# K and V loads of an attention decode kernel, each made as two DMAs of 64 partitions

## The chip, the cores and the metric

The kernel runs on one core of one Trainium2 chip. The metric is the time of one execution on the device in microseconds (us); of several runs the median is given. A profiled execution has a time of its own, and its span (from the first to the last instruction) is a little shorter than that time.

The core has five engines that run side by side and wait for one another by semaphores: TensorE (PE, its weight loads PEld), VectorE (DVE), ScalarE (ACT), GpSimd (POOL) and SyncE (SP). In this kernel SyncE does nothing but wait and issue transfers. The transfers are done by 16 DMA engines, which move data from the main memory (HBM) to the on-chip memory (SBUF). SBUF has 128 partitions.

## The reference

The inputs are one token for each of 8 sequences (x, 640 wide), a cache of 4096 keys and values for each of 32 heads (128 wide), and weights. What is computed, in short:

```python
xn = layernorm(x)
q  = (xn @ wq) as 32 heads of 128
scores = einsum("bhqd,bhkd->bhqk", q, k_cache) * 128 ** -0.5
o  = einsum("bhqk,bhkd->bhqd", softmax(scores), v_cache) @ wo
y  = layernorm(xn)
h  = gelu(y @ w1 + b1)
out = x + o + (h @ w2 + b2)
```

All tensors are bfloat16. The two caches are 8 x 32 x 4096 x 128 values each, 268 MB a cache; everything else is small beside them.

## The kernel before, in words

The work is cut into 32 tiles. A tile is one sequence with 8 of the 32 heads; `i` counts the tiles. For a tile, the keys of 8 heads are laid on the 128 partitions: 16 partitions for a head, and on each partition 256 keys of 128 values, 65,536 bytes that lie in one piece in HBM. `cache_src` makes this view of the cache. So the K load of a tile is one DMA of 128 rows of 64 KB (8.39 MB), and its V load is another.

SBUF holds three such tiles, the three slots of `S_sb`: K loads go to slots `KA` and `KB` in turn, V loads always to `VS`. Each slot has one load semaphore, `ld_s[s]`. A DMA adds 16 to its semaphore when all of it has landed; the helper `_Dma.sig` counts these 16 and returns the ticket (semaphore and value) for which a reader waits.

What is done with a tile:

- K: for 176 of the 256 keys of a partition, VectorE multiplies the keys by the query in place, folds them once and sums them, in three chunks (`dve_chunk`). For the other 80 keys TensorE transposes them, ScalarE copies the result out of PSUM, and TensorE multiplies it by the query (`pe_T`, `act_T`, `pe_QK`); VectorE picks out the right head (`dve_sel`). TensorE does not wait for the load itself: GpSimd waits (`k_ready`) and writes a small flag, `kr_sb`, whose ticket TensorE waits for.
- Then VectorE takes the maximum of each head (`dve_max`), and ScalarE makes the 8 exponentials (`act_exp`).
- V: TensorE multiplies the 256 slices of V by the probabilities (`pe_PV`), one tile behind.

SyncE issues the loads in the order of the positions in `at`: K of the next tile at `o - 51`, V of this tile at `o + 50` (lines 871 and 872), so K and V in turn. Ahead of a load, SyncE waits until its slot is free. In `load_k` (line 368) that is, from tile 6 on, the end of the exponentials of tile i - 2. In `load_v` (line 383) it is the end of the PV matmuls of tile i - 1. All loads from SyncE go through one queue. The V load of the last tile but one (i = 30) is made in two pieces along the keys, cut at 192 of 256 (`V_CUT`); the second piece has a semaphore of its own, `ld_vl`, for which `pe_PV` waits ahead of slice 192.

The program first records the calls of every engine in a list and then emits them, VectorE, ScalarE and TensorE as loops, in which the values they wait for grow by a constant step from turn to turn. Line 111 emits every instruction, which is why the profile gives that line for all of them.

Ahead of the first tile come the load of wq (into slot `VS`), two layer norms and the query. Behind the last K tiles, the weights of the MLP and wo are loaded into the K slots, and the products with them are added up in one PSUM bank.

Of the kernel before, what the change touches and what calls it, by code (L numbers as in the profile page):

```python
# [14 lines left out]
P = 128  # L15
# [177 lines left out]
def bass_parallel_sum__gqa_block_cached__mixer_channel_mlp__decode_kernel(  # L193
# [19 lines left out]
    NKEY = SK * HS // P  # L213
# [21 lines left out]
    KA, KB, VS = 0, 1, 2  # L235
# [2 lines left out]
    NL = 3  # L238
    WN_CUT = (0, 5 * CT, 7 * CT, 7 * CT + CT // 2, HS * CT)
    V_CUT = (0, 192, 256)  # L240

    def jp_of(i):
        return 80
# [6 lines left out]
    def kslot(i):  # L250
        return KA if i % 2 == 0 else KB
# [8 lines left out]
    with ExitStack() as es:  # L260
# [5 lines left out]
        tile = [S_sb[:, s, :].rearrange("p (j d) -> p j d", d=DH) for s in range(3)]  # L266
# [6 lines left out]
        def scratch(n, rows=P, slot=KB):  # L273
# [73 lines left out]
        pe, dve, act, sp, pool = (_Eng(sem(f"{n}_s")) for n in ("pe", "dve", "act", "sp", "pool"))  # L347
        pe2, act2, fin, fin2 = (_Eng(sem(n)) for n in ("pe2_s", "act2_s", "fin_s", "fin2_s"))
        ld_s = [_Dma(sem(f"ld_s{s}")) for s in range(3)]
        ld_x, ld_b1, ld_b2, ld_wq, ld_w1, ld_w2a, ld_w2b, st_a, st_o = (  # L350
            _Dma(sem(n)) for n in ("ld_x", "ld_b1", "ld_b2", "ld_wq", "ld_w1", "ld_w2a", "ld_w2b", "st_a", "st_o"))
        ld_vl = [_Dma(sem(f"ld_vl{q}")) for q in range(1, len(V_CUT) - 1)]
        ld_wl = [_Dma(sem(f"ld_wl{q}")) for q in range(2)]
        ld_wn = [_Dma(sem(f"ld_wn{q}")) for q in range(len(WN_CUT) - 1)]
        tk = {}
# [8 lines left out]
        def cache_src(cache, i):  # L364
            hq, b = divmod(i, B)
            return cache[b, hq * HS:(hq + 1) * HS].rearrange("h (p j) d -> (h p) j d", j=NKEY)

        def load_k(i):
            s = kslot(i)
            if i >= KLATE:  # L370
                sp.wait(tk[("exp", i - 2)])
            elif i >= 2:
                sp.wait(tk[("kt", i - 2)], tk[("km", i - 2)])
            elif s == KB:
                sp.wait(tk["qT"])
            tk[("k", i)] = ld_s[s].sig(sp.dma_start(tile[s], cache_src(A_k_cache, i)))

        def load_mlp():
            sp.wait(tk[("kt", NQ - 2)], tk[("km", NQ - 2)])
# [3 lines left out]
        def load_v(i):  # L383
            sp.wait(tk["qmm"] if i == 0 else tk[("pv", i - 1)])
            if i != NQ - 2:
                tk[("v", i)] = [ld_s[VS].sig(sp.dma_start(tile[VS], cache_src(A_v_cache, i)))]
                return
            tk[("v", i)] = []
            for d, lo, hi in zip([ld_s[VS]] + ld_vl, V_CUT[:-1], V_CUT[1:]):
                if lo:  # L390
                    d.n += 1
                tk[("v", i)].append(
                    d.sig(sp.dma_start(tile[VS][:, lo:hi, :], cache_src(A_v_cache, i)[:, lo:hi, :])))

# [324 lines left out]
        def pe_PV(i):  # L719
            PVB.use(pe)  # L720
            pe.wait(tk[("exp", i)])
            for j in range(NKEY):
                if j == 0:
                    pe.wait(tk[("v", i)][0])
                elif j in V_CUT:
                    pe.wait_ge(ld_vl[V_CUT.index(j) - 1].sem, 1)
                last = pe.matmul(PV_ps[:, 0:HS], tile[VS][:, j, :], P_sb[:, :, j],
# [114 lines left out]
        at(NQ * Q - 55, load_mlp)  # L842
        at(NQ * Q - 54.9, load_w2b)
        at(-870, load_k, 0)
        at(NQ * Q - 60.1, zero_w2b)
        at(-800, consts_pool)
# [20 lines left out]
        for i in range(NQ):  # L867
            o = i * Q
            last = i == NQ - 1
            if i:  # L870
                at(o - 51, load_k, i)
            at(o + 50, load_v, i)
            at(o - 52, qrep, i)
            at(o - 2, k_ready, i)
            at(o - 11, pe_qbc, i)
            at(o - 10.5, act_qbc, i)
            nt = jp_of(i) // TPB
            w = 42.0 / nt
            for t in range(nt):
                at(o + w * t, pe_T, i, t)  # L880
                at(o + w * (t + 0.4), act_T, i, t)
                at(o + w * (t + 1.5), pe_QK, i, t)
            at(o + 2, dve_chunk, i, 0)
            at(o + 26, dve_chunk, i, 1)
            at(o + 52, dve_sel, i, 0)
            at(o + 55, dve_sel, i, 1)
            at(o + 58, dve_chunk, i, 2)
            at(o + 84, dve_max, i)
            at(o + 90 if i else o + Q + 45, act_exp, i)
            at(o + Q + 48, pe_RS, i)  # L890
            at(o + Q + 57, dve_rinv, i)
            at(o + Q + 50, pe_PV, i)
            if not last:
                at(o + Q + 71, act_O, i)
            at(o + Q + 75, o_norm, i)
# [81 lines left out]
```

## Time and profile before

| what | value |
|---|---|
| time, median of 3 runs | 1281.42 us (1281.33 to 1281.44) |
| time of the profiled execution | 1281.24 us |
| its span | 1279.9 us |
| SyncE's waits ahead of V loads, for the PV matmuls | 785.6 us in 31 waits |
| SyncE's waits ahead of K loads, for the exponentials | 310.3 us in 26 waits |
| GpSimd's flag, waiting for K loads | 295.2 us in 31 waits |
| PV matmuls, waiting for V loads | 138.3 us in 30 waits |
| VectorE, waiting for K loads | 126.9 us in 28 waits |
| K load, from issue to landing | 26.1 to 39.1 us, median 38.8 |
| V load, from issue to landing | 24.7 to 52.6 us, median 31.6 |

How to read it: in the profile's names, `S_sb<-in_A_k_cache_dram` is a K load into one of the slots, `S_sb<-in_A_v_cache_dram` a V load, and `SPq` is SyncE's sequencer as it issues. The DMA row has one digit for each fortieth of the span, in tenths of busy time. "q1" is the DMA queue that SyncE fills, and its share is the time of its packets as a share of 16 DMA engines' span; a packet's time holds the time in which it is under way. A wait is put down to what ended last.

### The profile page before, as it was taken

What the parts mean: (1) busy time and instruction counts of PE and PEld (TensorE: products, weight loads), DVE (VectorE), ACT (ScalarE), POOL (GpSimd) and SP (SyncE); (2) the same over time, 40 slices, a digit from 0 to 9 for tenths busy, and PEclk for the clock granted to TensorE, in tenths of its full rate; (3) what the DMA queues carried; (4) which work ended last, traced back from release to release, by engine and by line L of the source; (5) the groups of instructions that cost most, each with busy time, mean ns of one, the idle gap of its engine ahead of it and who ended that gap; (6) DMA issues with size and microseconds to landing.
All of it is one profiled execution on the core that took longest, in us unless ns stands there. A gap on an engine that the chain in (4) does not pass through costs nothing.

```text
span 1279.9 us, 34138 instructions
## 1 busy us (share of the span) xinstructions
PE 672.1 (53%) x13794; PEld 570.6 (45%) x13794; DVE 1103.0 (86%) x684; ACT 476.5 (37%) x906; POOL 109.6 (9%) x121
## 2 busy tenths in 40 slices
PE   2536555446645446545456554456454466464476
PEld 0435444435535345444345444345343355353465
DVE  2899998889888889888899888898888898888894
ACT  0524444233444233443234443234443334442331
POOL 0020010000000000000000000000000000000050
PEclk8656655565565556555555555555565556655665
DMA  9999999999999999999999999999999999999998
GB/s 424 425 431 429 434 434 428 440 434 430 432 438 428 438 432 432 434 432 434 430 440 430 432 434 438 428 432 436 430 438 432 432 432 440 426 434 436 426 444 365
DMA packets 10784, 551.97 MB, mean 431 GB/s; under 512 B 1242, under 2 KB 1523, under 8 KB 1812
## 3 DMA queue, kind: packets, MB, share of 16 engines
q1 hardware_dynamic: 10736, 551.79, 99.7%
q8 instruction: 8, 0.13, 0.0%
q14 instruction: 4, 0.03, 0.0%
q10 hardware_dynamic: 36, 0.02, 0.0%
HBM read 551.80 MB, written 0.01 MB: 431 GB/s over the span
## 4 chain that ended last, share of the span: by engine, by line
DMA 46%; DVE 37%; issue 12%; ACT 4%; PE 1%; DVEq 0%; SPq 0%
DMA S_sb<-in_A_k_cache_dram 42%; DVE S_sb L111 26%; DVE Sd_sb L111 8%; ACT P_sb L111 4%; DMA S_sb<-in_B_w_dram 2%; DMA S_sb<-in_A_wo_dram 2%; DVE S_ps L111 1%; PE TR_ps L111 1%; DVE mx_sb L111 1%; DVE mxT_sb L111 0%; DVE mbT_sb L111 0%; DVEq L109 0%; DVE mq_sb L111 0%; DVE NB_sb L111 0%; DVE ri_sb L111 0%
## 5 line engine op out<-in xcount | busy, mean ns | idle before, releaser
L111 PE MATMUL TR_ps<-ident_bf,S_sb 128*128 128x128 bf16 (+1 forms) x2578 | 341.8, 279 | 354.1 <-POOL kr_sb L111 331.4
L111 DVE TENSOR_TENSOR S_sb<-S_sb,qbc_sb 128x7552 bf16<-128x7552 bf16 (+1 forms) x96 | 388.8, 4050 | 127.2 <-DMA S_sb<-in_A_k_cache_dram 126.9
L111 PEld LDWEIGHTS TR_ps<-ident_bf,S_sb 128*128 (+2 forms) x2578 | 245.1, 103 | 412.4 <-issue 339.6
L111 DVE TENSOR_REDUCE Sd_sb<-S_sb 128x59 f32<-128x3776 bf16 (+1 forms) x96 | 390.2, 4065 | 6.0
L111 ACT ACTIVATE KT_sb<-TR_ps 128x1024 bf16<-128x1024 bf16 x320 | 326.6, 1023 | 120.5 <-PE TR_ps L111 109.4
L111 PE MATMUL PV_ps<-P_sb,S_sb 128*128 128x8 bf16 x8192 | 224.0, 175 | 141.3 <-DMA S_sb<-in_A_v_cache_dram 138.3
L111 PEld LDWEIGHTS PV_ps<-P_sb,S_sb 128*128 128x128 bf16 x8192 | 221.4, 103 | 144.1 <-DMA S_sb<-in_A_v_cache_dram 141.0
L111 DVE TENSOR_TENSOR S_sb<-S_sb 128x3776 bf16<-128x3776 bf16 (+1 forms) x96 | 206.5, 2151 | 3.3
L111 ACT ACTIVATE P_sb<-Sd_sb,NB_sb 128x256 bf16<-128x256 f32 x256 | 126.3, 494 | 210.1 <-DVE NB_sb L111 210.1
L111 PE MATMUL S_ps<-qrep_sb,KT_sb 128*128 128x8 bf16 x2560 | 121.9, 177 | 50.3 <-ACT KT_sb L111 47.0
L111 ACT ACTIVATE oU_sb<-PV_ps 128x8 f32<-128x8 f32 x31 | 5.5, 177 | 377.5 <-PE PV_ps L111 377.5
L111 PEld LDWEIGHTS S_ps<-qrep_sb,KT_sb 128*128 128x128 bf16 x2560 | 91.8, 103 | 82.2 <-ACT KT_sb L111 40.0
L111 POOL TENSOR_TENSOR oT_sb<-oU_sb,ri_sb 128x8 bf16<-128x8 f32 x31 | 71.5, 2306 | 371.4 <-DVE S_sb L111 315.3
L111 POOL COPY qrep_sb<-qT_sb 128x128 bf16<-128x128 bf16 x32 | 18.5, 578 | 470.0 <-PE S_ps L111 453.3
L111 ACT ACTIVATION_READ_ACCUMULATOR P_sb<-Sd_sb,NB_sb 128x1 f32 x256 | 47.7, 186 | 0.0
L111 DVE TENSOR_TENSOR S_ps<-S_ps,mask_sb 128x320 f32<-128x320 f32 (+1 forms) x65 | 31.6, 486 | 2.7 <-PE S_ps L111 2.7
L111 DVE TENSOR_REDUCE Sd_sb<-S_ps 128x40 f32<-128x320 f32 x64 | 31.5, 492 | 2.2
L111 ACT ACTIVATE qbc_sb<-QB_ps 128x128 bf16<-128x128 f32 x32 | 8.9, 277 | 58.2 <-PE QB_ps L111 58.2
L111 PE MATMUL QB_ps<-ident_bf,qrep_sb 128*128 128x128 bf16 x32 | 9.1, 283 | 40.2 <-DVE S_sb L111 21.9
L111 POOL MEMSET kr_sb<- 128x1 f32 x32 | 3.1, 98 | 295.2 <-DMA S_sb<-in_A_k_cache_dram 295.2
L111 PEld LDWEIGHTS QB_ps<-ident_bf,qrep_sb 128*128 128x128 bf16 x32 | 3.3, 103 | 43.1 <-ACT oU_sb L111 29.1
L111 PE MATMUL CH_ps<-rs_sb,ones_f 128*128 128x8 f32 x64 | 16.2, 326 | 6.1 <-ACT P_sb L111 6.1
(70 smaller groups left out, 150.1 us busy)
## 6 DMA issues: line engine op xcount, KB each, us to landing
S_sb<-in_A_v_cache_dram SPq DMA_DIRECT2D x1, 6144.0 KB, 26.8
S_sb<-in_A_wq_dram SPq DMA_DIRECT2D x1, 5120.0 KB, 15.2
S_sb<-in_A_wo_dram SPq DMA_DIRECT2D x1, 2560.0 KB, 18.4
S_sb<-in_B_w_dram SPq DMA_DIRECT2D x1, 2160.0 KB, 30.3
S_sb<-in_B_w_dram SPq DMA_DIRECT2D x1, 2080.0 KB, 34.8
S_sb<-in_A_v_cache_dram SPq DMA_DIRECT2D x1, 2048.0 KB, 31.3
S_sb<-in_A_wo_dram SPq DMA_DIRECT2D x1, 1280.0 KB, 21.1
S_sb<-in_A_wo_dram SPq DMA_DIRECT2D x1, 800.0 KB, 22.6
```

The costliest lines, as they stand in the source:

```text
L111: inst = getattr(e, name)(*a, **k)
```

## The change

Each K load and each V load becomes two DMAs, the first for partitions 0 to 63 (the first four heads of the tile), the second for partitions 64 to 127 (the other four). Both add 16 to the slot's semaphore, and `load_rows` returns the ticket of the second, so readers wait for both. The two are issued one after the other by SyncE, with no wait between them. Of the V load of tile 30, the first piece (keys 0 to 191 of a partition) is made as two DMAs too; the second piece stays one DMA of 128 partitions. Nothing else is changed.

```diff
+    PH = P // 2
...
+        def load_rows(s, cache, i, lo, hi):
+            for r in range(0, P, PH):
+                t = ld_s[s].sig(sp.dma_start(
+                    tile[s][r:r + PH, lo:hi, :], cache_src(cache, i)[r:r + PH, lo:hi, :]))
+            return t
+
         def load_k(i):
             s = kslot(i)
...
-            tk[("k", i)] = ld_s[s].sig(sp.dma_start(tile[s], cache_src(A_k_cache, i)))
+            tk[("k", i)] = load_rows(s, A_k_cache, i, 0, NKEY)
...
         def load_v(i):
             sp.wait(tk["qmm"] if i == 0 else tk[("pv", i - 1)])
             if i != NQ - 2:
-                tk[("v", i)] = [ld_s[VS].sig(sp.dma_start(tile[VS], cache_src(A_v_cache, i)))]
+                tk[("v", i)] = [load_rows(VS, A_v_cache, i, 0, NKEY)]
                 return
-            tk[("v", i)] = []
-            for d, lo, hi in zip([ld_s[VS]] + ld_vl, V_CUT[:-1], V_CUT[1:]):
-                if lo:
-                    d.n += 1
+            tk[("v", i)] = [load_rows(VS, A_v_cache, i, 0, V_CUT[1])]
+            for d, lo, hi in zip(ld_vl, V_CUT[1:-1], V_CUT[2:]):
+                d.n += 1
                 tk[("v", i)].append(
                     d.sig(sp.dma_start(tile[VS][:, lo:hi, :], cache_src(A_v_cache, i)[:, lo:hi, :])))
```

## The prediction

> **What bounds the kernel now.** I read first the head of the page and its DMA rows, to see whether any compute engine or the transfers fill the span.
>
> ```profile
> span 1279.9 us, 34138 instructions
> PE 672.1 (53%) x13794; PEld 570.6 (45%) x13794; DVE 1103.0 (86%) x684; ACT 476.5 (37%) x906; POOL 109.6 (9%) x121
> ...
> DMA  9999999999999999999999999999999999999998
> ...
> DMA packets 10784, 551.97 MB, mean 431 GB/s; under 512 B 1242, under 2 KB 1523, under 8 KB 1812
> ...
> q1 hardware_dynamic: 10736, 551.79, 99.7%
> ```
>
> No slice of the DMA row falls below 8 tenths, and the one queue that SyncE fills (q1) has packets under way for 99.7% of the time of 16 DMA engines. All bytes go through it. VectorE, the busiest engine, has 86% of the span, so it has room; the transfers have none. Next, the VectorE timeline: the first multiply of each tile waits for its K load, so three of these starts give the beat.
>
> ```profile
> 558.69 4.03 DVE L111 TENSOR_TENSOR S_sb<-S_sb,qbc_sb 128x7424 bf16<-128x7424 bf16 x1 [4.27 <-DMA S_sb<-in_A_k_cache_dram]
> ...
> 597.39 4.03 DVE L111 TENSOR_TENSOR S_sb<-S_sb,qbc_sb 128x7424 bf16<-128x7424 bf16 x1 [4.26 <-DMA S_sb<-in_A_k_cache_dram]
> ...
> 636.10 4.03 DVE L111 TENSOR_TENSOR S_sb<-S_sb,qbc_sb 128x7424 bf16<-128x7424 bf16 x1 [4.27 <-DMA S_sb<-in_A_k_cache_dram]
> ```
>
> The beat is 597.39 - 558.69 = 38.70 us and then 38.71 us. In it VectorE waits 4.27 us, and what it waits for is the transfer. The view of stretches (busy time of PE, PEld, VectorE, ScalarE and GpSimd, then granted clock, DMA share and GB/s) gives the same beat as a rate:
>
> ```profile
> 210.00:600.00 390.00, 205.68 (x4206) 175.39 (x4206) 341.27 (x201) 149.75 (x288) 27.30 (x31) 0.53 1.00 433
> 600.00:1180.00 580.00, 303.42 (x6283) 258.88 (x6282) 507.39 (x301) 220.29 (x420) 41.02 (x45) 0.55 1.00 434
> ...
> 558.69:597.39 38.70, 20.41 (x419) 17.51 (x419) 33.86 (x20) 14.72 (x28) 2.69 (x4) 0.50 1.00 434
> ```
>
> One K and one V load pass in a beat (2 x 128 rows of 65,536 bytes, 16.78 MB): 16.78 MB / 38.70 us = 433.5 GB/s, the last row's 434, and the long stretches before and after it have the same. One load therefore takes 19.35 us of the queue, VectorE has 33.86 us of work in 38.70, and the DMA share is 1.00. The queue is never empty, as SyncE's timeline shows:
>
> ```profile
> 585.00 0.33 SPq L111 DMA_DIRECT2D S_sb<-in_A_v_cache_dram  x1
> 597.23 0.33 SPq L111 DMA_DIRECT2D S_sb<-in_A_k_cache_dram  x1
> 623.71 0.33 SPq L111 DMA_DIRECT2D S_sb<-in_A_v_cache_dram  x1
> ```
>
> The K load issued at 597.23 is the one that lets VectorE start at 636.10, 38.9 us later: twice its own 19.35, because the V load of 585.00 is still passing. So each load waits behind another one, and the kernel is a stream of bytes at 433.5 GB/s with a short start and end.
>
> **The change part by part.**
>
> *Issues.* 32 K loads, 31 whole V loads and the first piece of the V load before the last become two DMAs each: 64 more.
>
> ```profile
> L111 SPq DMA_DIRECT2D S_sb<-in_A_k_cache_dram x32: 327/328/407, 1.2 to 1177.8; - x32
> L111 SPq DMA_DIRECT2D S_sb<-in_A_v_cache_dram x33: 327/328/434, 22.2 to 1238.2; - x33
> ```
>
> At 0.328 us each they take 64 x 0.328 = 21 us of SyncE, which has nothing else to do. The second half is issued 0.33 us after the first. It lies behind the first half in the queue, and the first half behind a load under way: at 623.71 the K load of 597.23 has still until about 636.0, so 12.3 us cover the 0.33. What stands behind the second issue in SyncE's order is the next load's wait, which ends over 12 us later. I cost the issues at nothing; uncovered they would be at most the 21 us.
>
> *Waits.* Both halves add 16 to the same semaphore, and the ticket handed on is that of the second. GpSimd's gate, VectorE and the PV matmuls wait for 32 where they waited for 16. No wait is new, none goes, and nothing starts at the first half: no gain is possible here. Each slot is loaded again only after its tile was used, so the counts cannot run ahead.
>
> *Closing entries.* The 65 K and V issues alone would give 65 x 16 = 1040 packets, if each ends with one mark for each of the 16 DMA engines, and I read most of the 1242 packets under 512 B as these. So the change adds about 64 x 16 = 1024 of them, 64 to an engine. No row has their time. Bound: at the beat's 433.5 GB/s the 551.97 MB take 1273.3 us, which leaves 1279.9 - 1273.3 = 6.6 us for the start, the end and all closings, at most 0.10 us for each of 65, so 0 to 6.5 us for 64. They cannot be below nothing. I take 1 us, nearer to nothing, since the start and the end have most of the 6.6: the first small load alone is used only 2.26 us into the span (row below).
>
> *The rate of a half.* This is the large term. Before, the 16 DMA engines together fill 128 partitions; after, all 16 fill partitions 0 to 63 with one half, and then 64 to 127 with the next, because the halves are one behind the other in the same queue. Same bytes, same rows of 64 KB, half the destinations at a time. The rate of 433.5 GB/s is 27.1 GB/s for a DMA engine and, equally, 3.39 GB/s for a partition, and the row does not say which of the two is the limit. The row of a narrower transfer doesn't either (the first row is for the sum below):
>
> ```profile
> S_sb<-in_A_v_cache_dram SPq DMA_DIRECT2D x1, 6144.0 KB, 26.8
> ...
> S_sb<-in_A_x_dram ACTq DMA_DIRECT2D x1, 10.0 KB
> ...
> 0.75 0.59 ACTq L111 DMA_DIRECT2D S_sb<-in_A_x_dram  x1
> ...
> 2.26 0.88 DVE L111 BATCH_NORM_STATS2 S_sb<-S_sb 8x6 f32<-8x320 bf16 x2
> ```
>
> This 10 KB load into 8 partitions is used 0.92 us after its issue ended, so each partition took at least 1.4 GB/s; nothing in the trace shows a partition that takes more than 3.39. Bounds: if the DMA engines are the limit, a half takes 9.68 us and the change costs nothing. If what the destinations take in is the limit, a half takes 19.35 us, and a load 38.7. Loads changed: 32 + 31 + 0.75 (6144 of 8192 KB) = 63.75, so the upper end is 63.75 x 19.35 = 1233.6 us. A gain is excluded by the 99.7% and the unchanged bytes. I take the upper end: it is the intake that the rows have shown (3.39 GB/s for a partition of a long load), while the lower end asks 6.8 GB/s of a partition, twice any row.
>
> [...]
>
> *Sum.* 1279.9 + 1233.6 + 1 = 2514.5 us span, and the profiled run took 1281.24, that is 1.34 us outside the span: 2515.8. The median of the three runs is 1281.42, 0.2 us above the profiled one; I say 2516. All compute is then covered twice over: a beat of 77.4 us holds VectorE's 33.86.
>
> **The rivals.**
>
> *The DMA engines are the limit: no change.* Each of the 16 moves 27.1 GB/s whatever the destination, and the memory takes it on half of its partitions. The mechanism sits in the q1 stream and decides from 6.8 GB/s for a partition: if one can take that, halves cost nothing. For it: the rate is the same 433 or 434 in every stretch of the stream, as a fixed rate of an engine would make it. Against: a fixed rate of the destinations would look the same. Time: 1281.2 + 1 = 1282 (1281 to 1288). The same time results if the change does not do what it says, and the two halves are dealt to different DMA engines, 8 to each, and pass side by side.
>
> *The engines fall out of step: in between.* Suppose that each DMA engine works through its own rows without waiting for the others. Of a half, each has 4 rows. If in each pair whose rows collide one gets these 4 rows (9.7 us) ahead, it writes to the upper half while the other writes to the lower, and nothing collides. For it: 12.3 us of queued work stand ahead at a V issue, enough for such a lead. Against: it needs something that favours one of two, and the trace, with one beat of 38.70 and 38.71, shows no drift. With half the overlap gone: 1281 + 617 + 1 = 1899; from 1290 to 2380.
>
> *SyncE becomes late.* The 21 us of issues would show at 1281 + 21 = 1302 at most; the 12.3 us of cover speak against it. I give it 0.01.
>
> *A gain.* Nothing starts earlier and no byte goes. 0.03, for an effect I don't see.
>
> **How the numbers follow.** Halves at half rate, 2380 to 2550: 0.45. Between, 1290 to 2380: 0.20. No change to 0.2%: 0.31. A gain of more: 0.03; SyncE 0.01. A measurement of this kernel can tell about 0.2%, 2.6 us, from no change. So faster 0.03, same 0.31, slower 0.66. The predicted time is the likeliest, 2516. Its own range, 2380 to 2550, holds less than half of the chance, and with the cases between it 0.65, under 8 in 10, so the range must reach down to the case without change: 1281 to 2550.
>
> **What would show it.** Right: the DMA share stays at 9 tenths and more with GB/s near 217; the beat between the first multiplies of successive tiles becomes 77 us; VectorE falls to some 45% of the span; the waits for K and V grow by over 30 us a tile. The engines as the limit: the beat stays 38.70, GB/s 434, and the only trace of the change is 64 more issue rows on SyncE and about 1000 more packets under 512 B. Between: the GB/s row climbs in the course of the span. If SyncE is late: slices with the DMA row under 9. The forecast is wrong if GB/s stays above 400.

## The result, and the profile after

The changed kernel takes 2619.41 us in the median of 6 runs (2614.62 to 2623.65), the kernel before 1281.38 us in the same series: a ratio of 2.0437, 95% interval 2.0411 to 2.0463. The profiled execution took 2623.65 us. The forecast was 2516, and its range ended at 2550. So the direction was right, and the price of a half was put 4% too low.

These lines of the page of the changed kernel answer to those of before:

```profile
span 2622.2 us, 34202 instructions
PE 673.2 (26%) x13794; PEld 572.2 (22%) x13794; DVE 1103.1 (42%) x684; ACT 473.6 (18%) x906; POOL 39.5 (2%) x121
...
DMA  9999999999999999999999999999999999999999
GB/s 254 203 204 209 208 208 207 210 207 208 207 210 207 208 206 209 207 208 206 210 206 208 208 208 208 208 208 208 208 208 208 208 208 208 208 208 208 208 226 258
DMA packets 11808, 551.98 MB, mean 210 GB/s; under 512 B 2266, under 2 KB 2547, under 8 KB 2836
...
q1 hardware_dynamic: 11760, 551.79, 100.0%
```

VectorE has the same 1103 us of work, in twice the span. The bytes are the same, and the packets under 512 B are 2266 - 1242 = 1024 more, as counted in the prediction. The DMA engines are as busy as before, and they move half. If DMA engines hold each other up at the destination (a collision, which the experiments test), it looks like this in the profile: the busy share of the DMA row does not show it, since a packet counts as busy for as long as it is under way; the GB/s row shows it. It is also flat from the second slice on, so the loss is there from the first K load and does not grow or heal.

VectorE's timeline gives the beat, again by the first multiply of successive tiles:

```profile
1228.48 4.02 DVE L111 TENSOR_TENSOR S_sb<-S_sb,qbc_sb 128x7424 bf16<-128x7424 bf16 x1 [46.31 <-DMA S_sb<-in_A_k_cache_dram]
1309.25 4.03 DVE L111 TENSOR_TENSOR S_sb<-S_sb,qbc_sb 128x7424 bf16<-128x7424 bf16 x1 [46.34 <-DMA S_sb<-in_A_k_cache_dram]
1390.01 4.03 DVE L111 TENSOR_TENSOR S_sb<-S_sb,qbc_sb 128x7424 bf16<-128x7424 bf16 x1 [46.32 <-DMA S_sb<-in_A_k_cache_dram]
```

The beat is 80.77 us, the wait in it 46.3 us where it was 4.27. A beat holds one K and one V load, so a load takes 40.38 us and a half 20.19. With 63.75 such loads, 1279.9 + 63.75 x (40.38 - 19.35) = 2620.6 us, and the span is 2622.2: this one term is the whole result.

### The profile page after: what moved, and what is told of

It is laid out like the page before. It is cut to its first block, busy times and chain, and to the rows that moved or that the text cites. A ratio compares the mean times of both kernels' runs of the same rounds, so it can differ in the third digit from the quotient of the medians.

```text
span 2622.2 us, 34202 instructions
## 1 busy us (share of the span) xinstructions
PE 673.2 (26%) x13794; PEld 572.2 (22%) x13794; DVE 1103.1 (42%) x684; ACT 473.6 (18%) x906; POOL 39.5 (2%) x121
## 2 busy tenths in 40 slices
DMA packets 11808, 551.98 MB, mean 210 GB/s; under 512 B 2266, under 2 KB 2547, under 8 KB 2836
## 4 chain that ended last, share of the span: by engine, by line
another core or an unknown queue 69%; PE 24%; DMA 3%; ACT 2%; issue 1%; POOL 0%; DVE 0%; SPq 0%; ACTq 0%
PE TR_ps L111 11%; PE PV_ps L111 9%; PE S_ps L111 4%; DMA S_sb<-in_A_v_cache_dram 2%; ACT KT_sb L111 2%; DMA S_sb<-in_A_wq_dram 1%; PE CH_ps L111 0%; POOL oT_sb L111 0%; ACT oU_sb L111 0%; PE ACC_ps L111 0%; ACT P_sb L111 0%; POOL kr_sb L111 0%; POOL qrep_sb L111 0%; DVE S_sb L111 0%
## 5 line engine op out<-in xcount | busy, mean ns | idle before, releaser
L111 POOL TENSOR_TENSOR oT_sb<-oU_sb,ri_sb 128x8 bf16<-128x8 f32 x31 | 7.1, 229 | 1018.1 <-ACT oU_sb L111 1018.1
L111 PEld LDWEIGHTS CH_ps<-rs_sb,ones_f 128*128 128x128 f32 x64 | 14.4, 279 | 5.7 <-issue 3.7
```

What stands on the lines that cost most here:

```text
L111: inst = getattr(e, name)(*a, **k)
```

## The experiments

The packets of the trace can be taken one by one. A row of a load (one partition's 64 KB) is one packet, so its time tells how fast one DMA engine writes one partition. In the table are the medians of all full rows, from the packet records of each run's trace, beside the times, for the runs with one kind of cut throughout; the runs follow one by one. By an end-mark, here and in the expectations, I mean one of the packets of 4 bytes of which the 64 added DMAs brought 1024, 16 for each DMA; I take it for the packet with which a DMA engine closes its part of a DMA.

```
run                          us        row of 64 KB, us
before                       1281.4    2.42
after: 0-63, 64-127          2619.4    5.12
key halves                   1286.3    1.216 (32 KB rows)
same source                  1286.3    1.216 (32 KB rows)
quarters: 0-31, 32-63, ...   2624.6    5.11
sixteen in a row             4700.3    9.12
even, odd                    1281.5    2.42
every eighth (16)            2614.3    5.07
every fourth of a half (16)  2613.0    5.07
```

### Two DMAs, cut along the keys

```diff
-            for r in range(0, P, PH):
-                t = ld_s[s].sig(sp.dma_start(
-                    tile[s][r:r + PH, lo:hi, :], cache_src(cache, i)[r:r + PH, lo:hi, :]))
+            m = (lo + hi) // 2
+            for a, b in ((lo, m), (m, hi)):
+                t = ld_s[s].sig(sp.dma_start(tile[s][:, a:b, :], cache_src(cache, i)[:, a:b, :]))
```

> Each load stays two DMAs on one semaphore, but cut along the keys: 128 partitions, 32 KB rows. As many DMAs and end-marks as in the changed kernel. Theory (64 partitions at a time collide at the destination): 1281 to 1288 us, beat 38.7 us, 433 GB/s. Rival (the number of DMAs, their issues or end-marks cost the time): near 2619 us, or at least over 1300.

Measured: 1286.3 us, ratio 1.0038 (1.0025 to 1.0052). As many DMAs, issues, end-marks and semaphore counts as in the changed kernel cost at most 5 us, not 1338. So their number is not the cause. The 5 us are looked at below, with the even and odd halves.

### The same source, all partitions

```diff
-            for r in range(0, P, PH):
-                t = ld_s[s].sig(sp.dma_start(
-                    tile[s][r:r + PH, lo:hi, :], cache_src(cache, i)[r:r + PH, lo:hi, :]))
+            hq, b = divmod(i, B)
+            n = (hi - lo) // 2
+            for h in range(2):
+                h0 = hq * HS + h * (HS // 2)
+                src = cache[b, h0:h0 + HS // 2].rearrange("h (p j) d -> (h p) j d", j=NKEY // 2)
+                t = ld_s[s].sig(sp.dma_start(tile[s][:, lo + h * n:lo + (h + 1) * n, :], src[:, 0:n, :]))
```

> The two DMAs of a load read the same halves of the cache as the changed kernel (four heads, then four heads, each 4.2 MB in one piece), but each lands on all 128 partitions, so the keys lie in another layout and the output is not that of the reference. Theory (destination): 1281 to 1288 us. Rival (16 DMA engines that read within 4.2 MB at a time get in each other's way at the source): near 2619 us.

Measured: 1286.28 us, ratio 1.0038 (1.0023 to 1.0053), the same as the key halves. Reading four heads, 4.2 MB in one piece, is no slower than reading eight. So the loss is not at the source, and the destination is left.

### The middle half, and two quarters

```diff
-            for r in range(0, P, PH):
+            for r, n in ((P // 4, PH), (0, P // 4), (3 * P // 4, P // 4)):
                 t = ld_s[s].sig(sp.dma_start(
-                    tile[s][r:r + PH, lo:hi, :], cache_src(cache, i)[r:r + PH, lo:hi, :]))
+                    tile[s][r:r + n, lo:hi, :], cache_src(cache, i)[r:r + n, lo:hi, :]))
```

> Three DMAs for a load: partitions 32 to 95 (64 of them), then 0 to 31, then 96 to 127. [...] Rival (any DMA of 64 partitions runs at half rate, any of 32 no faster): 2619 us or more. [...]

Measured: 2308.37 us in 2 runs (2295.73 and 2321.02), ratio 1.8015 (1.7924 to 1.8105): neither the 1281 of the kernel before nor 2619. The view of stretches of this run shows why (columns as in the prediction: busy time of five engines, clock, DMA share, GB/s):

```profile
14.80:24.00 9.20, 4.59 (x49) 1.87 (x49) 1.74 (x4) 0.28 (x1) 0.30 (x1) 0.92 0.94 406
25.00:44.00 19.00, 0.00 (x0) 0.00 (x0) 0.00 (x0) 0.00 (x0) 0.00 (x0) 0.50 0.85 183
45.00:54.00 9.00, 6.42 (x101) 5.48 (x102) 7.75 (x3) 5.94 (x7) 0.10 (x1) 0.74 0.85 359
300.00:800.00 500.00, 140.46 (x2920) 119.77 (x2917) 235.63 (x141) 100.97 (x196) 5.70 (x21) 0.53 0.88 231
```

The first row is the middle half of the first K load, the second its two quarters, the third the middle half of the next load: full rate, half, full. (In so short a stretch both GB/s and share come out low at the edges; GB/s divided by the share is 432, 215 and 422.) The packet records say it more plainly: in the first load all 16 DMA engines have four rows of about 2.42 us (one engine's fourth took 3.2) and then four of 4.4 to 5.1. So 64 partitions in a row are not slow as such; 32 to 95 run at full rate, 0 to 63 at half. Later in the stream (last row) the DMA engines are no longer in step, a middle half of some of them meets a quarter of others, and rows of up to 7.6 us appear. The first loads begin 29 to 31 us apart; over the whole stream a load takes 19.35 + (2308.37 - 1281.43) / 63.75 = 35.5 us. Longer rows are only a part of what is lost later: the DMA share of the last row is 0.88, and in the packet records most engines stand idle for some 5 to 16 us in a beat. A load counts as landed when its last engine is done, and SyncE issues the next V load only after the PV matmuls that wait for it, so the other engines run out of queued work. Being out of step costs here, where my rival of the prediction let it help.

### Quarters

```diff
-            for r in range(0, P, PH):
+            for r in range(0, P, P // 4):
                 t = ld_s[s].sig(sp.dma_start(
-                    tile[s][r:r + PH, lo:hi, :], cache_src(cache, i)[r:r + PH, lo:hi, :]))
+                    tile[s][r:r + P // 4, lo:hi, :], cache_src(cache, i)[r:r + P // 4, lo:hi, :]))
```

> Four DMAs of 32 partitions for a load, one behind the other. As the prediction put it, a limit of 3.39 GB/s for each partition: a quarter 19.35 us, a load 77.4 us, the whole 1281 + 63.75 x 58.05 = 4982 us. [...]

Measured: 2624.58 us, ratio 2.0482 (2.0445 to 2.052). The limit per partition, as the prediction put it, falls clearly: 32 partitions take in as much as 64. The view of stretches of this run has 208 GB/s (last column), as the changed kernel has.

```profile
200.00:1000.00 800.00, 202.27 (x4190) 171.82 (x4190) 332.42 (x199) 146.06 (x280) 8.16 (x30) 0.54 1.00 208
```

### Sixteen in a row

```diff
-            for r in range(0, P, PH):
+            for r in range(0, P, P // 8):
                 t = ld_s[s].sig(sp.dma_start(
-                    tile[s][r:r + PH, lo:hi, :], cache_src(cache, i)[r:r + PH, lo:hi, :]))
+                    tile[s][r:r + P // 8, lo:hi, :], cache_src(cache, i)[r:r + P // 8, lo:hi, :]))
```

> Eight DMAs of 16 partitions for a load, one behind the other. [...] If each added DMA costs 0.08 us as with the key halves, 448 of them add 34 us at most. Rival (DMAs under 128 partitions run at half rate, however many): 2620 to 2660 us.

Measured: 4700.26 us in one run, far over the rival's 2660. The rate does not follow the count of DMAs: the two runs at the end of this section also make eight DMAs of 16 partitions of a load, on other partitions, and have 209 GB/s. The page of this run:

```profile
GB/s 151 116 115 113 113 115 116 116 116 115 116 116 114 112 115 116 116 116 115 116 113 112 114 116 116 116 115 116 114 113 113 116 116 116 116 115 115 113 114 179
```

115 GB/s into 16 partitions are 7.2 GB/s for a partition, over twice the 3.39 of the prediction. A row takes 9.12 us, 3.77 times the 2.42 of before, where the halves have 2.11 times (5.12 us).

### The cut from tile 8 on, and 8 DMA engines four rows behind

```diff
...
+            if i < 8:
+                m = (lo + hi) // 2
+                parts = [(slice(0, P), a, b) for a, b in ((lo, m), (m, hi))]
+            else:
+                parts = [(slice(r, r + PH), lo, hi) for r in range(0, P, PH)]
+            if i == 8 and s != VS:      # only in the second of the two runs
+                parts = [(slice(j, P // 4, 4), lo, hi) for j in range(4)] + [(slice(P // 4, P), lo, hi)]
...
-        replay(nc.scalar, "act")
+        _replay(nc.scalar, act.calls)
```

In the first of the two runs the K load of tile 8 is cut along the keys like those before it. VectorE's loop is written out in the same way.

> The cut into 64 partitions only from the V load of tile 8 on; up to the K load of tile 8 the two DMAs are cut along the keys, on all 128 partitions. VectorE's and ScalarE's loops are written out, so that the counts of the semaphores may change on the way. 23 K loads and 23.75 V loads stay cut by partitions. Theory (a fixed price for each such load, 2 x 20.18 - 19.35 = 21.0 us): 1281 + 46.75 x 21.0 = 2263 us, and 433 GB/s up to tile 8, then 208. Rival (the price grows or falls in the course of the stream): over 2330 or under 2200.

Measured: 2256.88 us in 2 runs (2250.48 and 2263.28); 2263 was expected. The GB/s row of its page has the step at tile 8, and then a plain:

```profile
GB/s 416 427 433 431 432 434 238 214 211 211 213 208 212 211 212 213 209 206 216 209 212 209 211 211 207 212 211 207 210 207 211 210 209 211 206 209 210 210 226 207
```

So each load of two halves has a fixed price, (2256.88 - 1281.36) / 46.75 = 20.9 us, and it stays the same from tile 8 to the end.

> As the run from tile 8, but the K load of tile 8 is made as four DMAs of 8 partitions (every fourth of 0 to 31), which keep 8 of the 16 DMA engines busy for 4 rows, and one of the other 96 partitions: 8 engines are 4 rows behind the other 8 from there on, half of a load. Theory (two engines collide only where both are at the same half at once, and the lead stays): rows at full rate again, 1285 to 1350 us. [...] Rival 2 (the lead is lost at the next load for want of queued work): between, 1400 to 2200 us.

Measured: 2223.49 and 2291.88 us in two runs, 3% apart, one below and one above the first cut's 2256.88. The theory's 1285 to 1350 us are far off. The edit did what it should: in the packet records, eight of the 16 DMA engines begin the V load of tile 7 at 331 to 334 us of the span and the other eight at 353 to 354. The first group reaches the K load of tile 9 first, where its rows take up to 8.1 us as long as the other group still has its V load. From 399 to 410 us the first group is in the second half of that K load and the other group in the first, and the rows of both take 5.1 us all the same. A limit of each half of the partitions, whoever writes, does not fit this: eight engines with such rows bring 8 x 64 KB / 5.12 us = 102 GB/s into a half that takes 208 from 16. What keeps the rows at 5.1 us is not shown; nothing in the records names the engine of a packet.

The prediction's rival of engines that fall out of step finds a little support: after the step at tile 8 the GB/s row climbs from 206 to 230, where that of the first of the two runs stays at 206 to 216 in all but two slices, and in the packet records rows of 3.2 us appear late in the stream. A tenth of the rate is the most that it gains.

```profile
GB/s 415 431 429 431 434 342 215 206 216 216 217 210 214 216 214 219 212 219 214 216 214 218 217 222 225 227 227 227 227 225 228 229 227 230 227 224 217 219 218 205
```

### Even and odd partitions

```diff
-            for r in range(0, P, PH):
+            for r in range(2):
                 t = ld_s[s].sig(sp.dma_start(
-                    tile[s][r:r + PH, lo:hi, :], cache_src(cache, i)[r:r + PH, lo:hi, :]))
+                    tile[s][r:P:2, lo:hi, :], cache_src(cache, i)[r:P:2, lo:hi, :]))
```

> Two DMAs for a load, the even partitions and then the odd ones: 64 partitions each, spread over all 128. [...]

Measured: 1281.49 us in one run: neither the 2619 us of the lower and upper halves nor the 5 us that the key halves added. It was run again, eleven times:

> The even and odd halves once more, with rounds, for a ratio with an interval. If 64 added DMAs cost nothing and the 5 us of the key halves came from their 8064 added rows of half the length: within 0.05% of the kernel before, 1281.4 us. If the 5 us came from the 64 added DMAs: 1286 us.

Measured: 1281.51 us in 11 runs, ratio 1.0001 (0.9992 to 1.001). The page of that run:

```profile
GB/s 422 425 429 433 436 430 430 440 432 432 432 436 430 436 432 434 434 432 434 430 440 428 436 430 438 430 432 436 434 434 430 436 430 440 428 436 430 431 445 361
DMA packets 11808, 551.98 MB, mean 431 GB/s; under 512 B 2266, under 2 KB 2547, under 8 KB 2836
```

The packets are those of the changed kernel to the last one, 11808, and the rate is that of before. Here are two DMAs of 64 partitions, on one semaphore, one behind the other, with 4.2 MB in each: only which partitions make a half is another, and with it which rows of the cache are read first, which, as the run with the same source shows, is not what slowed the changed kernel. It also settles the 5 us of the key halves. The 64 added DMAs with their 1024 end-marks cost nothing that can be measured. The key halves had 8192 packets more than this run, 20000:

```profile
DMA packets 20000, 551.98 MB, mean 429 GB/s; under 512 B 2266, under 2 KB 2547, under 8 KB 2836
```

8192 / 16 = 512 rows more for a DMA engine, and 4.9 us / 512 = 9.6 ns a row. The rows of 32 KB took 1.216 us in the median and two of them 2.432, 10 ns over the 2.42 of a whole one.

### Every eighth, and every fourth of a half

```diff
-            for r in range(0, P, PH):
+            for r in range(8):
                 t = ld_s[s].sig(sp.dma_start(
-                    tile[s][r:r + PH, lo:hi, :], cache_src(cache, i)[r:r + PH, lo:hi, :]))
+                    tile[s][r:P:8, lo:hi, :], cache_src(cache, i)[r:P:8, lo:hi, :]))
```

> Eight DMAs of 16 partitions for a load, each every eighth of the 128 (0, 8, ... 120; then 1, 9, ...). With 16 rows each DMA engine has one row of a DMA, so it is known which 16 partitions are written at one time. [...] Map B (partitions 8 apart never meet, as the even and odd halves at full rate suggest, if each DMA engine has successive rows of a DMA): 1281 us and up to 3 us for 448 more DMAs.

Measured: 2614.28 us, ratio 2.0401 (2.0364 to 2.0439). Map B, in the expectation, is the supposition that partitions 8 apart do not slow one another; its 1281 us are far off. These 16 partitions stand as far apart as 16 can, and a row takes 5.07 us all the same. The view of stretches has the rate:

```profile
200.00:2400.00 2200.00, 554.24 (x11570) 473.02 (x11570) 926.70 (x552) 397.05 (x767) 21.90 (x82) 0.53 1.00 209
```

```diff
-            for r in range(0, P, PH):
-                t = ld_s[s].sig(sp.dma_start(
-                    tile[s][r:r + PH, lo:hi, :], cache_src(cache, i)[r:r + PH, lo:hi, :]))
+            for r in range(0, P, PH):
+                for j in range(4):
+                    t = ld_s[s].sig(sp.dma_start(
+                        tile[s][r + j:r + PH:4, lo:hi, :], cache_src(cache, i)[r + j:r + PH:4, lo:hi, :]))
```

> Eight DMAs of 16 partitions for a load, each every fourth of a half (0, 4, ... 60; ... then 64, 68, ... 124). [...] Rival (the row at a time is the limit only for neighbours under four apart, and 64 partitions in a row are slow for the order in which the engines get them): 1281 us.

Measured: 2613.0 us in one run, rows of 5.07 us, and not the 1281 us of the rival.

Every eighth at half rate and the even and odd halves at full rate leave a question. If each DMA engine had four successive rows of the 64 and wrote one after the other, the 16 even partitions written at one time would be 0, 8, ... 120, those of the run with every eighth, and the rows would take 5.07 us; in the packet records of the even and odd halves they take 2.42 us from the first K load on, where all 16 engines begin within 1.3 us. Yet four successive rows each would fit the lower half: there the 16 would be 0, 4, ... 60, those of the run with every fourth, and 5.12 us is near its 5.07. So either a DMA of 64 rows is dealt in another way, or an engine's successive rows overlap in time. How it is stays open. No run settles it.

## Why the prediction was right in its direction and wrong in its size and its reason

*What bounds the kernel* was right: a stream of bytes, with nothing else near. All that slowed the stream came out in the time one to one (2620.6 by the one term, 2622.2 measured).

*Issues, waits, closing entries* were right at nothing, nothing and 1 us: the even and odd halves have the same of all three and differ from before by 0.10 us, inside the interval. An issue of 64 partitions takes SyncE longer than the 0.328 us that I took from one of 128 (the view of the K loads of the changed kernel, min/median/max in ns), and it is hidden as argued:

```profile
L111 SPq DMA_DIRECT2D S_sb<-in_A_k_cache_dram x64: 465/570/1170, 1.2 to 2412.6; - x64
```

*The rate of a half* is the step that failed, in two ways. First its size: I put a half at 19.35 us, the exact double; it takes 20.19. So the term 63.75 x 19.35 = 1233.6 us of the sum measured 63.75 x 21.03 = 1340.7 (21.03 is 40.38 - 19.35), and these 107 us are what the span lacked in the forecast. The packet records show where: a row takes 5.12 us and not 4.84 (twice 2.42), except for one of four rows, mostly 4.85, where a DMA engine changes from one half to the next. So a row of a half takes 6% more than the double. The range ended at 2550 because I let a half cost little more than the double, and nothing in the trace of before showed more. Why the halves lose 6%, and sixteen in a row not (9.12 us, where four times 2.42 are 9.68), is open.

Second its reason. I took the upper end because no row showed a partition with more than 3.39 GB/s. That figure is a mean over 128 partitions, most of which wait at any time; a row of 2.42 us is 27.1 GB/s into one partition, and this was in the packet records of before. The quarters refute the limit per partition (2624.6 against 4982), and the even half takes the full rate with 64 (433 GB/s, where the lower half has 208). So what is limited is something that sets of partitions have in common; what it is, no run shows. That the forecast came near is in so far luck: for the lower and upper halves a limit per partition gives about what was measured, and for the quarters and the even half it does not.

*The lower end for the halves*, 2380, supposes that a pair of halves gains on the double; no run shows such a gain. What the runs showed in its place is a loss: a load of two halves took 40.38 us, 4% over the 38.7 of the double. The case in between, from 1290 to 2380, has its upper end from the same supposition. Nor is it the sharing of the DMA engines that costs the time: the key halves and the even and odd halves pass through the 16 DMA engines just as much, and cost 0.4% and nothing.

*The rivals.* That the DMA engines are the limit is wrong for this cut: 16 of them, with a DMA share of 1.00 in both, bring 208 GB/s into the halves and 434 into the even and odd ones. Whether they are the limit of the kernel before is not shown. That engines fall out of step and recover did not happen in the changed kernel, whose rows keep their 5.12 us to the end; in the run with the middle half they fell out of step and lost by it, and in the run with eight of them behind they gained a tenth of the rate at most. SyncE was not late, and there was no gain.

## What to carry to other kernels

Cut a load along the free dimension or by every other partition, not into lower and upper partitions: the even and odd halves cost nothing (1.0001) and the key halves 0.4%, the lower and upper ones twice the time (2.0437). When GB/s falls while the DMA share stays at 1.00, compare the time of single packets of equal size before and after, and ask which partitions are written at the same time. And do not read a rate divided by 128 as what one partition can take: here it was 3.39 GB/s, and one row brought 27.1 into one partition.

## What the runs showed of the hardware that I had not expected

Sixteen partitions, written by eight DMAs of 16, take 209 GB/s when they stand 8 or 4 apart and 115 when they are neighbours. And the price of a row does not rise steadily: 2.42 us into all partitions, 5.12 (2.11 times) into halves, 9.12 (3.77 times) into sixteen in a row.

An added row costs about 10 ns of a DMA engine (9.6 by the 4.9 us of the key halves), an added DMA none that could be measured: 64 of them, in a stream with a DMA share of 1.00, changed the time by a ratio of 1.0001.

GpSimd's small multiply of the output became ten times faster in the changed kernel, without any edit to it. The groups of the page, before and after:

```profile
L111 POOL TENSOR_TENSOR oT_sb<-oU_sb,ri_sb 128x8 bf16<-128x8 f32 x31 | 71.5, 2306 | 371.4 <-DVE S_sb L111 315.3
```

```profile
L111 POOL TENSOR_TENSOR oT_sb<-oU_sb,ri_sb 128x8 bf16<-128x8 f32 x31 | 7.1, 229 | 1018.1 <-ACT oU_sb L111 1018.1
```

In the trace of before, a multiply of VectorE (TENSOR_TENSOR) is under way at each of the 31, and GpSimd's ends 86 to 92 ns after VectorE's does, so that it takes between 1.3 and 3.9 us. Here is one of them:

```profile
585.24 2.12 DVE L111 TENSOR_TENSOR S_sb<-S_sb 128x3776 bf16<-128x3776 bf16 x1
585.26 2.19 POOL L111 TENSOR_TENSOR oT_sb<-oU_sb,ri_sb 128x8 bf16<-128x8 f32 x1 [12.12 <-DVE S_sb L111]
```

After, no multiply of VectorE is under way at any of the 31, and each takes 229 or 230 ns. So GpSimd's seems to wait for the end of VectorE's; no run changed that alone.
